# RWKV-6 state scan and gated FFN on one core: a new instruction order, with new bank, mask and transfer tables

## The chip, the cores and the metric

The kernel runs on one core of a Trainium2 chip. The metric is the time of the program on the device in microseconds; lower is better. Engines: PE is TensorE (matmuls; PEld is its weight load), DVE is VectorE, ACT is ScalarE, POOL is GpSimd, SP is SyncE, which here only issues transfers. POOL issues transfers too.

## The reference

The first half is a linear attention with a state of 48 x 48 per head, 4 batches, 8 heads, 768 steps; the second half a gated FFN without activation on 3072 rows.

```python
for t in range(S):
    cur = einsum('bhd,bhe->bhde', u[None] * kt, vt)
    y[:, :, t] = einsum('bhd,bhde->bhe', rt, state + cur)
    state = wt[:, :, :, None] * state + einsum('bhd,bhe->bhde', kt, vt)
# x: y as (3072, 384)
a = x @ w1          # 384 x 1024
b = x @ w2          # 384 x 1024
out = (a * b @ w3) @ w_out      # 1024 x 1024, 1024 x 384
```

## The kernel before

Time is cut into 6 chunks of 128 steps. A unit `t` is one chunk of one or two batches; there are 13: units 0 and 1 are chunk 0 of one batch each, unit 2 is chunk 0 of the other two batches, and units 3 to 12 are chunks 1 to 5 in pairs of batches. The steps of a unit, by the names of the order:

- `win`, `kin`, `rin`, `vin` load the rows of w, k, r and v. The transfers issued by POOL turn float32 into bfloat16 on the way (those of w do not). Unit 0 comes by SP into float32 tiles and is converted on chip (`kc`, `rc`, `vc`).
- `ln` and `cs` make the logarithm of w and its running sum over the chunk (a matmul with a triangle), `ne` and `e` the exponentials of it, `KRk` and `KRr` the scaled k and r. They are turned by 128 x 128 transposes on PE with an eviction (`trk` and `trke`, `trr` and `trre`) or by transposing transfers on SP (`dtk`, `dtr`). In the units of `RAW` (0, 1, 2, 3, 6) r is turned first (`trw`) and scaled by `KRw`, with factors made by `csT` and `et`.
- `m_t_b` multiplies turned k and r into a 128 x 128 score per head; the strict triangle is cut out by DVE from PSUM (`msk`), or, for the pairs in `POOL_MASK`, ACT copies (`mcp`) and POOL or DVE masks in SBUF (`maff`).
- The diagonal term is apart: `rk`, `ruk`, `dg` (sum over a head), `dv`. `ys` (state part) and `yi` (score part) sum into PSUM; `yb` adds `dv` and writes the rows of y. In the units of `Y_PE` a matmul `yd` adds `dv` and `ybc` copies.
- The rows are turned into `xT` by PE (`yt`, eviction `xT`) or, in `DMA_Y`, by two transposing transfers (`dty`).
- The state: `kv` is k times v, `T` adds the old state, `S` scales it by `pc`, `Sb` writes a bfloat16 copy. In `KV_WIDE` the product is made for pairs of heads, half as many matmuls, and `T` (or `S` in chunk 0) reads it in two halves of 64 partitions.

The FFN of a unit has four groups `g` (two for units 0 and 1): `a_t_g` and `b_t_g` are the matmuls with w1 and w2 (six of 256 columns), `asb` copies a to SBUF on ACT, `abT` multiplies by b from PSUM on DVE. Then `o_t_b` multiplies by w34 = w3 x w_out, `osb` evicts and `st` stores. w34 is made once on chip: `wt` turns w3, `w3Te` evicts, `wm` multiplies by w_out, `w34e` evicts. `warm` are matmuls on zeros. The rows of units 8 to 11 are loaded into the space of w3 and w_out once these are used up.

There is no scheduler: the text `ORDER` lists every step with its engine, `BANKS` gives each step its PSUM bank or its buffer, and the instructions of an engine stand in that order. Each engine works its own list in order and waits where an input or a buffer is not ready, and so do the queues: POOL's list has its transfers and its products, SP's list all stores and transposing transfers. Where a step of the order is a transfer, what stands behind it on that engine is issued later.

```python
ORDER = """
table@ACT zeros@DVE padlw@DVE win_0@POOL ones@DVE LT@POOL ln_0@ACT warm0@17 cs_0@PE ne_0@ACT win_1@POOL win_2@POOL
"""
```

Of the kernel before, what the change touches and what calls it, by code (L numbers as in the profile page):

```python
# [41 lines left out]
tk1=3 m1_0=0,1 M1_0=3 y1=0,1 yt1=2 kv1=3 a1_0=0 b1_0=6 sa1_0=0 a1_1=3 b1_1=2 sa1_1=1 o1_0=7 so1_0=2 cs2=0,1 ct2=3,4
tr2=5 tk2=6 m2_0=0,1 M2_0=1 m2_1=0,1 M2_1=2 y2=6,7 yt2=2 kv2=3 a2_0=5 b2_0=6 sa2_0=0 a2_1=7 b2_1=1 sa2_1=0 a2_2=5
b2_2=0 sa2_2=1 a2_3=7 b2_3=1 sa2_3=2 o2_0=5 so2_0=3 o2_1=6 so2_1=1 cs3=4,5 ct3=4,5 tr3=5 tk3=4 m3_0=2,3 M3_0=0
m3_1=4,5 M3_1=1 y3=0,1 yt3=0 kv3=2 a3_0=5 b3_0=6 sa3_0=2 a3_1=6 b3_1=7 sa3_1=2 a3_2=6 b3_2=4 sa3_2=1 a3_3=3 b3_3=2
sa3_3=0 o3_0=7 so3_0=2 o3_1=4 so3_1=0 cs4=4,5 tr4=4 tk4=5 m4_0=2,3 M4_0=2 m4_1=0,1 M4_1=3 y4=4,5 kv4=0,1 a4_0=4 b4_0=6
sa4_0=0 a4_1=2 b4_1=5 sa4_1=0 a4_2=7 b4_2=4 sa4_2=2 a4_3=0 b4_3=7 sa4_3=1 o4_0=5 so4_0=2 o4_1=4 so4_1=2 cs5=2,3 tr5=7
tk5=3 m5_0=2,3 M5_0=1 m5_1=6,7 M5_1=0 y5=0,1 yt5=6 kv5=6 a5_0=6 b5_0=7 sa5_0=0 a5_1=6 b5_1=2 sa5_1=0 a5_2=4 b5_2=1
sa5_2=2 a5_3=0 b5_3=2 sa5_3=1 o5_0=2 so5_0=3 o5_1=0 so5_1=0 cs6=0,1 ct6=0,1 tr6=0 tk6=1 m6_0=2,3 M6_0=3 m6_1=0,1
M6_1=2 y6=3,4 yt6=3 kv6=5 a6_0=5 b6_0=3 sa6_0=2 a6_1=3 b6_1=5 sa6_1=2 a6_2=4 b6_2=3 sa6_2=0 a6_3=0 b6_3=4 sa6_3=0  # L50
o6_0=0 so6_0=0 o6_1=3 so6_1=1 cs7=2,3 tk7=1 m7_0=2,3 M7_0=1 m7_1=6,7 M7_1=0 y7=0,1 yt7=1 kv7=5 a7_0=1 b7_0=5 sa7_0=2
# [12 lines left out]
kin_2@POOL padkr@DVE csT_0@PE rin_0@SP padr@DVE I128@POOL rin_2@POOL rin_1@POOL rc_0@ACT trw_0@PE et_0@ACT kin_0@SP  # L64
kc_0@DVE KRk_0@DVE ln_1@ACT mask1@DVE warm7@2 csT_1@PE pc_0@ACT rk_0@DVE cs_1@PE ne_1@ACT padet@DVE KRw_0@DVE ln_2@ACT
pc_1@ACT trk_0@PE trke_0@DVE kin_1@POOL warm7@2 m_0_0@PE u@SP csT_2@PE cs_2@PE w3_0@POOL vin_0@SP vc_0@DVE kv_0@PE
mcp_0_0@ACT ne_2@ACT uc@DVE ruk_0@DVE dg_0@DVE S_0@DVE rk_2@DVE mask@POOL vin_2@POOL w2_0@POOL KRk_2@DVE trw_2@PE
et_2@ACT dv_0@DVE KRw_2@DVE trk_2@PE trke_2@ACT KRk_1@DVE warm7@5 m_2_0@PE maff_0_0@DVE yi_0_0@PE yd_0@PE ruk_2@DVE
wt_0_0@PE wt_0_1@PE dg_2@DVE et_1@ACT wt_1_0@PE pc_2@ACT mcp_2_0@ACT maff_2_0@DVE trk_1@PE trke_1@DVE w1_1@POOL
vin_1@POOL m_2_1@PE trw_1@PE w2_1@POOL w1_0@POOL kv_2@PE wt_1_1@PE w3Te_0@ACT ybc_0@ACT w3Te_1@ACT win_3@POOL yt_0@PE  # L70
msk_2_1@DVE yi_2_0@PE yi_2_1@PE dv_2@POOL yd_2@PE ybc_2@ACT KRw_1@DVE m_1_0@PE xT_0@DVE rk_1@DVE wo@POOL ruk_1@POOL
b_0_0@PE yt_2@PE warm5@2 a_0_1@PE asb_0_1@ACT msk_1_0@DVE xT_2@DVE b_2_0@PE S_2@DVE yi_1_0@PE a_2_2@PE dg_1@DVE
w3_1@POOL dv_1@DVE a_2_3@PE yb_1@DVE yt_1@PE kv_1@PE xT_1@DVE b_2_2@PE asb_2_2@ACT abT_2_2@DVE b_2_1@PE b_1_1@PE
asb_2_3@ACT ln_3@ACT b_0_1@PE abT_0_1@DVE S_1@DVE a_1_0@PE a_0_0@PE asb_0_0@ACT abT_0_0@DVE a_2_0@PE asb_2_0@ACT
abT_2_0@DVE a_1_1@PE a_2_1@PE asb_1_1@ACT asb_2_1@ACT kin_3@POOL cs_3@PE abT_2_1@DVE ne_3@ACT b_1_0@PE wm_1@PE
asb_1_0@ACT b_2_3@PE abT_2_3@DVE Sb_0@DVE rin_3@POOL csT_3@PE et_3@ACT wt_2_0@PE wt_2_1@PE wt_3_0@PE pc_3@ACT
abT_1_0@DVE wm_0@PE wt_3_1@PE KRk_3@DVE trk_3@PE w3Te_2@DVE abT_1_1@DVE trw_3@PE KRw_3@DVE wm_2@PE w3_2@POOL Sb_1@DVE
w34e_1@ACT rk_3@DVE trke_3@ACT ruk_3@DVE m_3_0@PE msk_3_0@DVE m_3_1@PE w3Te_3@ACT wm_3@PE w34e_3@ACT vin_3@POOL
w34e_0@DVE wt_5_0@PE wt_4_0@PE wt_4_1@PE wt_5_1@PE ys_3@PE w3Te_5@ACT kv_3@PE yi_3_0@PE w34e_2@DVE w3Te_4@DVE wm_4@PE
w34e_4@ACT msk_3_1@DVE yi_3_1@PE dg_3@DVE dv_3@DVE yb_3@DVE wm_5@PE win_4@POOL ln_4@ACT w3_3@POOL wt_6_0@PE iw_4@ACT  # L80
Sb_2@ACT w34e_5@ACT wt_6_1@PE w3Te_6@DVE wt_7_0@PE wt_7_1@PE cs_4@PE e_4@ACT yt_3@PE w3Te_7@DVE xT_3@DVE T_3@DVE
wm_6@PE ne_4@ACT win_5@POOL kin_4@POOL S_3@DVE wm_7@PE ln_5@ACT cs_5@PE w34e_6@DVE a_3_1@PE pc_4@ACT iw_5@ACT
w34e_7@ACT KRk_4@DVE trk_4@PE e_5@ACT ne_5@ACT rin_4@POOL rw_4@DVE KRr_4@DVE trr_4@PE vin_4@POOL kv_4@PE rk_4@DVE
ruk_4@DVE asb_3_1@ACT dg_4@DVE o_0_0@PE o_2_1@PE T_4@DVE pc_5@ACT rin_5@POOL S_4@DVE kin_5@POOL trke_4@ACT trre_4@ACT
m_4_1@PE osb_0_0@ACT st_0_0@SP m_4_0@PE msk_4_0@DVE msk_4_1@DVE ys_4@PE win_6@POOL ln_6@ACT kin_6@POOL rin_6@POOL
vin_5@POOL KRk_5@DVE rk_5@DVE rw_5@DVE osb_2_1@ACT o_1_0@PE osb_1_0@ACT b_3_3@PE win_8@POOL vin_6@POOL dv_4@POOL
KRr_5@DVE yi_4_0@PE a_3_3@PE asb_3_3@ACT win_7@POOL win_9@POOL st_1_0@SP cs_6@PE ne_6@ACT Sb_3@ACT a_3_2@PE yi_4_1@PE
asb_3_2@ACT yb_4@DVE dty_4_1@SP b_3_1@PE trk_5@PE KRk_6@DVE abT_3_1@DVE csT_6@PE et_6@ACT kin_7@POOL pc_6@ACT rk_6@DVE
rin_7@POOL abT_3_3@DVE b_3_0@PE trke_5@ACT b_3_2@PE a_3_0@PE asb_3_0@ACT abT_3_0@DVE ruk_6@POOL trr_5@PE trre_5@ACT
trw_6@PE trk_6@PE o_2_0@PE m_5_1@PE m_5_0@PE KRw_6@DVE trke_6@ACT m_6_1@PE abT_3_2@DVE o_3_1@PE ruk_5@POOL dg_5@DVE  # L90
osb_2_0@ACT msk_5_1@DVE kv_6@PE kv_5@PE mcp_5_0@ACT m_6_0@PE mcp_6_1@ACT maff_5_0@DVE kin_8@POOL rin_8@POOL
msk_6_0@DVE ys_5@PE ln_7@ACT iw_7@ACT maff_6_1@POOL T_5@DVE T_6@DVE ln_8@ACT osb_3_1@ACT dv_5@POOL vin_7@POOL
vin_8@POOL o_3_0@PE dg_6@DVE osb_3_0@ACT cs_7@PE e_7@ACT dty_4_0@SP b_4_0@PE yi_5_0@PE yi_5_1@PE yb_5@DVE ne_7@ACT
pc_7@ACT win_11@POOL KRk_7@DVE a_4_0@PE asb_4_0@ACT dv_6@DVE b_4_1@PE a_4_2@PE Sb_4@ACT asb_4_2@ACT abT_4_0@DVE
cs_8@PE a_4_1@PE pc_8@ACT ys_6@PE b_4_3@PE yi_6_0@PE yt_5@PE e_8@ACT rw_7@DVE S_5@DVE KRr_7@DVE dtr_7@SP S_6@DVE
ne_8@ACT xT_5@ACT KRk_8@POOL a_4_3@PE yi_6_1@PE asb_4_3@ACT rk_7@DVE trk_7@PE win_10@POOL a_5_0@PE yb_6@DVE a_5_3@PE
b_4_2@PE rin_9@POOL asb_4_1@ACT abT_4_1@DVE yt_6@PE kin_9@POOL abT_4_3@DVE iw_8@ACT st_3_0@SP asb_5_0@ACT a_5_1@PE
# [692 lines left out]
```

## Time and profile before

| what | value |
|---|---|
| median of 3 runs | 164.85 us (164.43 to 165.8) |
| the profiled execution's own time | 164.84 us |
| its span | 163.1 us |
| granted TensorE clock | 1.0 |
| PE, DVE, ACT, POOL busy | 154.6, 125.2, 100.5, 97.8 us |
| HBM read, written | 27.98 MB, 4.72 MB |

The profile is of one execution. A row of the timeline gives start, time, engine, line and operation; neighbours of one kind are merged (x and their count), and the bracket behind it is idle time of the engine ahead of it with what ended it. A row of the chain gives start, time and what ran or was waited for. A PE matmul's time holds its way through the array, so its rate is read from the starts of a run of matmuls. The rows of DMA issues end with the microseconds from issue to landing.

### The profile page before, as it was taken

The numbers are of one execution on the slowest core, as the hardware profiler recorded it, in microseconds if no ns is written. First come the engines' busy times: TensorE is split into PE (matmuls) and PEld (weight loads), VectorE is DVE, ScalarE is ACT, GpSimd is POOL, SyncE is SP. The second block draws the span as 40 slices with busy tenths as digits, with TensorE's granted clock in tenths as the row PEclk, the third lists the DMA queues.
The fourth block names the chain that finished last, engine by engine and source line by source line (L and its number), as shares of the span: only waits on it lengthen the run. The fifth ranks groups of instructions, "written<-read, shape, count | busy, mean of one in ns | idle before, by whom it ended". The sixth has DMA issues, their size and how long they took to land.

```text
span 163.1 us, 4587 instructions
## 1 busy us (share of the span) xinstructions
PE 154.6 (95%) x1922; PEld 117.4 (72%) x1922; DVE 125.2 (77%) x202; ACT 100.5 (62%) x166; POOL 97.8 (60%) x90
## 2 busy tenths in 40 slices
PE   6977999999999999999999999999999999999990
...
GB/s 119 216 154 184 195 193 244 207 171 212 238 153 174 164 216 244 124 113 83 148 225 99 175 188 147 169 171 144 186 162 158 158 170 95 87 55 45 55 147 96
DMA packets 98837, 25.63 MB, mean 157 GB/s; under 512 B 90880, under 2 KB 96640, under 8 KB 98816
## 3 DMA queue, kind: packets, MB, share of 16 engines
...
q8 instruction: 15, 0.25, 0.7%
...
HBM read 27.98 MB, written 4.72 MB: 200 GB/s over the span
## 4 chain that ended last, share of the span: by engine, by line
PE 65%; DVE 14%; DMA 13%; issue 3%; POOL 2%; ACT 1%; DVEq 0%; POOLq 0%; ACTq 0%
PE banks L714 25%; PE banks L730 16%; DMA wo_bf<-in_moe_w_out_dram 8%; PE banks L380 7%; DMA win<-in_w_dram 5%; PE banks L551 3%; DVE dv L539 3%; DVE yb L614 2%; PE banks L371 2%; PE banks L596 2%; DVE abT L724 2%; PE banks L424 2%; PE banks L512 2%; PE banks L667 2%; DVE Mbf L570 1%
## 5 line engine op out<-in xcount | busy, mean ns | idle before, releaser
L714 PE MATMUL banks<-xT,w_bf 128*128 128x256 bf16 (+1 forms) x624 | 69.2, 264 | 0.7 <-DVE yb L614 0.4
L714 PEld LDWEIGHTS <-w_bf 128*128 128x128 bf16 x624 | 55.3, 98 | 8.2 <-issue 1.0
L719 ACT COPY a_sb<-banks 128x512 f32<-128x512 f32 x48 | 27.9, 589 | 25.8 <-PE banks L714 19.0
L724 DVE TENSOR_TENSOR abT<-a_sb,banks 128x512 bf16<-128x512 f32 x48 | 31.6, 682 | 14.9 <-ACT a_sb L719 7.9
L730 PE MATMUL banks<-w,abT 128*128 128x384 bf16 x192 | 33.8, 326 | 0.0
L730 PEld LDWEIGHTS <-abT 128*128 128x128 bf16 x192 | 18.2, 98 | 10.9
L570 DVE TENSOR_TENSOR Mbf<-banks,mask 128x1024 bf16<-128x1024 f32 x15 | 18.1, 1220 | 2.1 <-PE banks L551 2.1
L335 POOL DMA_DIRECT2D win<-in_w_dram x13 | 14.8, 1143 | 5.3 <-ACT NEt L441 3.2
L735 ACT COPY osb<-banks 128x384 f32<-128x384 f32 x21 | 10.0, 482 | 12.8 <-PE banks L730 12.8
L408 ACT ACTIVATE lw<-win 128x768 bf16<-128x768 f32 (+1 forms) x13 | 10.4, 796 | 8.5 <-DMA win<-in_w_dram 8.5
L530 DVE TENSOR_REDUCE dg<-ruk 128x16 f32<-128x768 bf16 (+1 forms) x13 | 11.5, 886 | 0.8 <-POOL ruk L524 0.7
L565 POOL TENSOR_SCALAR_AFFINE_SELECT Mbf<-Mbf 128x1024 bf16<-128x1024 bf16 x5 | 5.5, 1090 | 11.0 <-ACT Mbf L557 11.0
L380 PE MATMUL banks<-wo_bf,w3T 128*128 128x384 bf16 x64 | 11.6, 326 | 0.1
L335 POOL DMA_DIRECT2D kin<-in_k_dram x8 | 9.1, 1133 | 4.1 <-DMA win<-in_w_dram 2.8
L614 DVE TENSOR_TENSOR yb<-banks,dv 128x768 bf16<-128x768 f32 (+1 forms) x11 | 10.1, 919 | 1.8 <-PE banks L596 1.3
L441 ACT ACTIVATE NEt<-banks 128x768 bf16<-128x768 f32 (+1 forms) x13 | 9.9, 764 | 1.5 <-PE banks L424 1.1
L308 PE MATMUL banks<-zeros 128*128 128x512 bf16 x28 | 9.4, 488 | 1.3 <-DVE zeros L249 1.3
L335 POOL DMA_DIRECT2D rin<-in_r_dram x8 | 9.0, 1124 | 2.1 <-DMA w_bf<-in_moe_w_dram 1.5
L557 ACT CAST Mbf<-banks 128x1024 bf16<-128x1024 f32 x9 | 9.0, 1011 | 0.6 <-PE banks L551 0.5
L335 POOL DMA_DIRECT2D vin<-in_v_dram x8 | 9.2, 1148 | 0.2
L524 POOL TENSOR_TENSOR ruk<-rk,u_bc 128x768 bf16<-128x768 bf16 (+1 forms) x4 | 5.8, 1450 | 5.7 <-DVE rk L520 5.7
L380 PEld LDWEIGHTS <-w3T 128*128 128x128 bf16 x64 | 5.8, 98 | 3.6 <-DMA wo_bf<-in_moe_w_out_dram 0.2
(100 smaller groups left out, 244.9 us busy)
## 6 DMA issues: line engine op xcount, KB each, us to landing
out_dram<-osb SPq DMA_DIRECT2D x24, 192.0 KB, 3.9
...
kin<-in_k_dram POOLq DMA_DIRECT2D x7, 192.0 KB, 11.3
rin<-in_r_dram POOLq DMA_DIRECT2D x7, 192.0 KB, 11.2
vin<-in_v_dram POOLq DMA_DIRECT2D x7, 192.0 KB, 10.1
...
```

The source lines that it names most:

```text
L335: QUEUE[eng].dma_start(dst, src)
L380: nc.tensor.matmul(one(f"wm{fi}")[:, :DM], lhsT=w3T[fi % 2][:, gi, :], rhs=wo_bf[:, gi, :], start=(gi == 0), stop=(gi == FI - 1))
L408: nc.scalar.activation(LW[:, :, :D], ww, Act.Ln)
L441: nc.scalar.activation(N_.rearrange("t (b h) d -> t b (h d)", b=nb), cs_view(), Act.Exp, scale=-1.0)
L530: nc.vector.reduce_sum(dgs, ruks, axis=AX.X)
L570: nc.vector.tensor_mul(Mbf[bank[f"M{t}_{b}"]], mview(), mask.rearrange("s (j q) t -> s j q t", j=2))
L614: nc.vector.tensor_add(ybs.rearrange("t b (q e d) -> t e (b q) d", e=2, d=D), yview().rearrange("t e (x d) -> t e x d", d=D), dvs.rearrang ...
L714: nc.tensor.matmul(o[:, f, :], lhsT=wt[:, di, fi * P:(fi + 1) * P], rhs=x[:, di, :T], start=(di == 0), stop=(di == DI - 1))
L719: copier(eng)(a_sb[bank[f"sa{t}_{g}"]], one(f"a{t}_{g}"))
L724: nc.vector.tensor_mul(ab[:, g * per:(g + 1) * per, :T], sa.rearrange("p (f t) -> p f t", t=T), one(f"b{t}_{g}").rearrange("p (f t) -> p f ...
L730: nc.tensor.matmul(one(f"o{t}_{b}")[:, :DM], lhsT=ab[:, fi, b * C:(b + 1) * C], rhs=w34[:, fi, :], start=(fi == 0), stop=(fi == FI - 1))
L735: copier(eng)(osb[bank[f"so{t}_{b}"]], one(f"o{t}_{b}")[:, :DM])
```

## The change

Only the tables at the head of the kernel change; no step computes anything else.

```diff
-DMA_Y = {4, 9, 10, 11, 12}
+DMA_Y = {6, 8, 9, 10, 11, 12}
-POOL_MASK = {(0, 0), (2, 0), (5, 0), (6, 1), (7, 1), (9, 0), (10, 0), (11, 1), (12, 1)}
-Y_PE = {0, 2}
-KV_WIDE = {4}
+POOL_MASK = {(2, 1), (5, 1), (7, 0), (8, 1), (11, 1), (12, 0)}
+Y_PE = set()
+KV_WIDE = {1, 4, 10}
-wt0=5 wm0=1 wt1=2 wm1=3 wt2=7 wm2=6 wt3=0 wm3=0 wt4=3 wm4=3 wt5=7 wm5=7 wt6=6 wm6=1 wt7=3 wm7=7 cs0=0 ct0=0 tr0=1
+wt0=0 wm0=3 wt1=2 wm1=1 wt2=0 wm2=7 wt3=6 wm3=2 wt4=4 wm4=4 wt5=3 wm5=7 wt6=2 wm6=2 wt7=3 wm7=2 cs0=0 ct0=6 tr0=1
...
-table@ACT zeros@DVE padlw@DVE win_0@POOL ones@DVE LT@POOL ln_0@ACT warm0@17 cs_0@PE ne_0@ACT win_1@POOL win_2@POOL
+table@ACT zeros@DVE padlw@DVE padkr@DVE win_0@POOL ones@DVE ln_0@ACT LT@POOL win_2@POOL warm0@17 cs_0@PE rin_2@POOL
...
```

Steps that change their engine: from DVE to POOL `KRk_5`, `KRk_11`, `KRk_12`, `KRr_10`, `S_3`, `S_5`, `S_8`, `dv_6`, `dv_11`, `ruk_2`, `ruk_9`, `ruk_11`, `rk_11`, `rw_7`, `rw_9`, `rw_10`; from POOL to DVE `KRk_8`, `KRk_9`, `KRr_8`, `KRr_12`, `S_7`, `dv_2`, `dv_4`, `ruk_1`, `ruk_5`, `ruk_6`, `rk_12`, `rw_11`; from POOL to SP `win_9`, `win_10`, `win_11`; from ACT to POOL `rc_0`. Between ACT and DVE some evictions change sides: `osb` on DVE are 7 for 3, `w34e` 6 for 3, `Sb` 4 for 2, `xT` 2 for 6. DVE has 18 `msk` for 15 and 2 `maff` for 4.

POOL's list in the head (`kin_68` is `kin_1`, `w_bf` of 128x3x512 are the halves of w1 at L346 and of w2 at L350, `vin_73` is `vin_1`, `win_81` is `win_3`):

```order
+L335 DMA kin_68<-in_k_dram 128x8x48
+L346 DMA w_bf<-in_moe_w_dram 128x3x512 x2
 L350 DMA w_bf<-in_moe_w_dram 128x3x512
-L346 DMA w_bf<-in_moe_w_dram 128x3x512
+L524 TENSOR_TENSOR ruk_104<-rk_102,u_bc 128x768
+L565 AFFINE_SELECT Mbf_100<-Mbf_100 128x1024
 L335 DMA vin_73<-in_v_dram 128x8x48
 L350 DMA w_bf<-in_moe_w_dram 128x3x512
-L346 DMA w_bf<-in_moe_w_dram 128x3x512
 L335 DMA win_81<-in_w_dram 128x16x48
-L539 TENSOR_TENSOR dv_108<-vin_74,dg_106 128x768
 L354 DMA wo_bf<-in_moe_w_out_dram 128x8x384
```

Both halves of w1 now stand ahead of both of w2, and ahead of `vin_1`, the second transfer of w2, `win_3` and `wo` POOL has `ruk_2` and `maff_2_1`, where it had `dv_2` ahead of `wo` alone.

POOL's list where units 7 and 8 begin, before (`KR_94` are `KRk_8` and `KRr_8`, `ruk_104` is `ruk_8`; `w_bf` and `wo_bf` as targets are rows of later units):

```order
L335 DMA wo_bf<-in_v_dram 128x16x48
L335 DMA win_81<-in_w_dram 128x16x48
L445 TENSOR_TENSOR KR_94<-w_bf,NEt_90 128x16x48
L335 DMA win_80<-in_w_dram 128x16x48
L335 DMA w_bf<-in_r_dram 128x16x48
L335 DMA w_bf<-in_k_dram 128x16x48
L486 TENSOR_TENSOR KR_94<-rw_86,Et_88 128x16x48
L524 TENSOR_TENSOR ruk_104<-rk_102,u_bc 128x768
```

And of the change (`dv_108` is `dv_6`, `rw_87` is `rw_7`, `ruk_104` is `ruk_8`, `Sst_118` is `S_5`):

```order
L335 DMA win_78<-in_w_dram 128x16x48
L335 DMA wo_bf<-in_v_dram 128x16x48
L539 TENSOR_TENSOR dv_108<-vin_72,dg_106 128x768
L478 TENSOR_TENSOR rw_87<-rin_64,iw_85 128x768
L524 TENSOR_TENSOR ruk_104<-rk_102,u_bc 128x768
L689 TENSOR_TENSOR Sst_118<-Tst_116,pc_113 128x384
```

`KRk_8` and `KRr_8` are gone from POOL, and four products of units 5 to 8 stand there without a transfer between them.

DVE's list ahead of unit 6's scores, before (`abT_132` are unit 3's groups, `KRT_96` is `KRw_6`, `dg_107` is `dg_5`, `Mbf_98` is `msk_5_1`, `Mbf_99` `maff_5_0`, `Mbf_101` `msk_6_0`):

```order
L724 TENSOR_TENSOR abT_132<-a_sb_126,banks 128x512
L724 TENSOR_TENSOR abT_132<-a_sb_128,banks 128x512
L470 TENSOR_TENSOR KRT_96<-banks,ETt_92 128x1024
L724 TENSOR_TENSOR abT_132<-a_sb_127,banks 128x512
L530 TENSOR_REDUCE dg_107<-ruk_105 128x16
L570 TENSOR_TENSOR Mbf_98<-banks,mask 128x1024
L563 TENSOR_TENSOR Mbf_99<-Mbf_99,mask 128x1024
L570 TENSOR_TENSOR Mbf_101<-banks,mask 128x1024
```

And of the change (`yb_110` is `yb_4`, `Mbf_98` `msk_5_0`, `KRT_96` at L516 `trke_6` and at L470 `KRw_6`, `Mbf_100` and `Mbf_101` `msk_6_1` and `msk_6_0`):

```order
L614 TENSOR_TENSOR yb_110<-banks,dv_108 128x2x8x48
L724 TENSOR_TENSOR abT_132<-a_sb_127,banks 128x512
L570 TENSOR_TENSOR Mbf_98<-banks,mask 128x1024
L724 TENSOR_TENSOR abT_132<-a_sb_126,banks 128x512
L516 COPY KRT_96<-banks 128x1024
L470 TENSOR_TENSOR KRT_96<-banks,ETt_92 128x1024
L530 TENSOR_REDUCE dg_107<-ruk_105 128x16
L570 TENSOR_TENSOR Mbf_100<-banks,mask 128x1024
L570 TENSOR_TENSOR Mbf_101<-banks,mask 128x1024
```

`trke_6` and a third mask stand in this piece where ACT and a mask in SBUF had been, and `KRw_6` has more ahead of it.

More of the change, by code (lines that the diff above doesn't have):

```diff
@@ L42 @@
[L42 to L51, printed above, removed]
@@ L61 @@
 """
 ORDER = """
-table@ACT zeros@DVE padlw@DVE win_0@POOL ones@DVE LT@POOL ln_0@ACT warm0@17 cs_0@PE ne_0@ACT win_1@POOL win_2@POOL
[L64 to L97, printed above, removed]
@@ new lines @@
+padet@DVE KRw_0@DVE trke_0@ACT warm7@2 m_0_0@PE ln_2@ACT cs_2@PE ne_2@ACT csT_2@PE pc_2@ACT ruk_0@DVE dg_0@DVE
+vin_0@SP vc_0@DVE kv_0@PE msk_0_0@DVE KRk_2@DVE w1_1@POOL et_2@ACT ln_1@ACT trw_2@PE KRw_2@DVE warm4@2 trk_2@PE
+rk_2@DVE cs_1@PE yi_0_0@PE dv_0@DVE trke_2@ACT warm4@3 m_2_0@PE yb_0@DVE S_0@DVE m_2_1@PE w1_0@POOL wt_0_0@PE
+msk_2_0@DVE w2_1@POOL trw_1@PE ruk_2@POOL dg_2@DVE ne_1@ACT mcp_2_1@ACT csT_1@PE et_1@ACT Sb_0@ACT maff_2_1@POOL
+yt_0@PE xT_0@ACT yi_2_0@PE kv_2@PE KRk_1@DVE trk_1@PE trke_1@ACT wt_1_0@PE wt_1_1@PE w3Te_1@ACT yi_2_1@PE KRw_1@DVE
```

123 lines of the change are left out of this document (81 added, 42 removed).

## The prediction

> **What bounds the kernel now.** First the page's shares and its slices of TensorE (PE):
>
> ```profile
> PE 154.6 (95%) x1922; PEld 117.4 (72%) x1922; DVE 125.2 (77%) x202; ACT 100.5 (62%) x166; POOL 97.8 (60%) x90
> PE   6977999999999999999999999999999999999990
> ```
>
> PE is busy from slice 5 to the end. Then the table by stage (columns: the stretch, its length, busy time of PE, PEld, DVE, ACT and POOL, the granted clock, DMA share, GB/s):
>
> ```profile
> 33.40:53.82 20.42, 20.42 (x263) 15.20 (x264) 17.76 (x30) 13.83 (x23) 12.94 (x12) 1.00 1.99 190
> 53.82:74.00 20.18, 20.18 (x299) 15.45 (x297) 17.77 (x25) 17.12 (x28) 16.24 (x14) 1.00 1.83 167
> 74.00:84.30 10.30, 9.82 (x155) 8.28 (x153) 10.26 (x15) 8.23 (x16) 7.74 (x7) 1.00 1.38 161
> ```
>
> The clock is full, so no clock term is needed. From 33.40 on PE first idles in 74 to 84.3, where VectorE (DVE) is busy 10.26 of 10.30 us. The chain that ended last, a few pieces of it:
>
> ```profile
> 20.23 13.12 DMA wo_bf<-in_moe_w_out_dram
> ...
> 62.98 1.97 PE banks L714 x18
> ...
> 70.72 0.20 PE banks L586 x16
> ...
> 97.22 0.33 PE banks L633 x6
> ...
> 130.78 3.06 DVE dv L539
> ...
> 140.25 7.37 PE banks L714 x66
> 147.62 1.30 PE banks L730 x8
> ```
>
> It runs through the landing of `wo` at 33.35, then PE, then DVE up to 140 and PE to the end. But a piece of the chain is no loss: PE had other work beside that 3.06 of DVE. What PE lost is read from its starts. One L714 matmul takes 1.97/18 = 0.109 us, so a group of six 0.66; a `yt` takes 0.33, a `ys` 0.20, an `o` 1.30.
>
> ```profile
> 79.80 1.47 PE L714 MATMUL banks<-xT,w_bf 128*128 128x256 bf16 x12
> 81.64 0.81 PE L714 MATMUL banks<-xT,w_bf 128*128 128x256 bf16 x6 [0.37 <-DVE yb L614]
> 82.29 0.50 PE L633 MATMUL banks<-I,yb 128*128 128x128 bf16 x6
> 82.91 0.81 PE L714 MATMUL banks<-xT,w_bf 128*128 128x256 bf16 x6
> ...
> 134.51 0.37 PE L586 MATMUL banks<-Sbf,KRT 64*128 64x48 bf16 x16
> 135.03 2.78 PE L714 MATMUL banks<-xT,w_bf 128*128 128x256 bf16 x24
> ...
> 138.05 3.13 PE L714 MATMUL banks<-xT,w_bf 128*128 128x256 bf16 x25
> ```
>
> 79.80 + 12 x 0.109 = 81.11, but the next starts at 81.64: 0.53 lost. 82.29 + 0.33 against 82.91: 0.29. 134.51 + 0.20 against 135.03: 0.32. 138.05 + 1.97 for three groups against 140.25, where the chain goes on: 0.23. Together **1.37 us**, nearly all that waits cost behind 40 us. Ahead of them stand two stretched DVE instructions:
>
> ```profile
> L689 DVE TENSOR_TENSOR Sst<-Tst,pc x5: 552/557/1997, 50.2 to 87.1; 128x384 f32<-128x384 f32 x5
> 78.08 1.76 POOL L445 TENSOR_TENSOR KR<-w_bf,NEt 128x768 bf16<-128x768 bf16 x1 [1.91 <-ACT NEt L441]
> 131.37 1.63 POOL L520 TENSOR_TENSOR rk<-rin,kin 128x768 bf16<-128x768 bf16 x1
> 138.19 0.96 DVE L539 TENSOR_TENSOR dv<-vin,dg 128x768 bf16<-128x768 bf16 x1
> ```
>
> `S_6` (L689, at 78.3) needs 0.55 us and took 2.00 while GpSimd (POOL) ran `KRk_8`; `dv_11` took 3.06 while POOL ran `rk_12`, where another `dv` takes 0.96. I call this a port wait: 1.45 and 2.1 us of DVE.
>
> **Part 1: the head, to 39.1 us: 0.** Unit 2's rows go ahead of unit 1's and `w1` ahead of `w2`, but the set of transfers ahead of `wo` on POOL's queue is the same, and the three behind it (`w3_1`, `kin_3`, `rin_3`) are the same too. `wo` needed 13.12 us from issue to landing; its own 1024 x 384 values of two bytes are 4.1 us at the stage's 190 GB/s. The rest is backlog, so its landing follows the sum of bytes, not the order. Behind it:
>
> ```profile
> 24.08 1.16 POOL L335 DMA_DIRECT2D rin<-in_r_dram  x1
> rin<-in_r_dram POOLq DMA_DIRECT2D x1, 192.0 KB, 14.5
> 38.66 0.62 PE L465 MATMUL banks<-I,rin 128*128 128x128 bf16 x8
> 39.11 1.46 PE L380 MATMUL banks<-wo_bf,w3T 128*128 128x384 bf16 x8
> ```
>
> `rin_3` lands at 24.08 + 14.5 = 38.6; `trw_3` starts at 38.66, and `wm_2` behind it at 39.11. Both orders have the same PE work ahead of `wm_2`, but for `yd_0`, `yd_2`, one warm-up matmul and half of `kv_1`'s matmuls, under 1 us, which the changed kernel saves. As `trw_3` starts with the landing, that saving is swallowed. Nothing can be gained here unless bytes move faster; what can be lost is rival D. `rc_0` on POOL stands in no row: it costs between nothing, under the backlog, and about one POOL product (1.6); I take nothing, as 5 us and more of backlog stand behind it. `S_1` in two halves costs DVE at most one more `S` (0.55), and as the head ends with a landing this is nothing.
>
> **Part 2: PE's own work behind 39.1: -0.3.** `yt_6` and `yt_8` go, since these units' rows now come by transfers, and `yt_4` returns: one `yt` less, 0.33. `kv_10` in 8 wide matmuls for 16 narrow ones is about even.
>
> **Part 3: the waits named above: -1.4.** `KRk_8` leaves POOL and `dv_11` leaves DVE, so neither pair can meet again. The gain is less only if other pairs take their place (rival C).
>
> **Part 4: DVE from 53 to 71 us: +1.0.** DVE gets three masks more (two `maff` fewer), four `osb` more, three `w34e` more and a second half of `T_10`, against four `xT` and several products fewer: by row durations some 3.5 us more behind the first `wm`. Spread over 120 us this is nothing, but it is not spread. Rows for the sum:
>
> ```profile
> L570 DVE TENSOR_TENSOR Mbf<-banks,mask 128x1024 bf16<-128x1024 f32 x15 | 18.1, 1220 | 2.1 <-PE banks L551 2.1
> 62.44 0.55 DVE L445 TENSOR_TENSOR KR<-kin,NEt 128x768 bf16<-128x768 bf16 x1
> 62.91 0.68 DVE L724 TENSOR_TENSOR abT<-a_sb,banks 128x512 bf16<-128x512 f32 x1
> 63.50 0.55 DVE L520 TENSOR_TENSOR rk<-rin,kin 128x768 bf16<-128x768 bf16 x1
> ```
>
> Back to back, the next starts 0.08 before the end (62.44 to 62.91, 62.91 to 63.50): 0.47 for a product, 0.60 for an `abT`, and so 1.14 for a mask and 0.88 for a `dv`, as which I count `dg` and `yb` too. From `T_3` to `KRw_6` the changed order has 3 masks, 4 `abT`, `dg_4`, `dv_4`, `yb_4`, `trke_6` and `KRw_6` (taken as `abT`) and 13 of the size of a product: 3.4 + 2.4 + 2.6 + 1.2 + 6.1 = 15.7 us. PE from `m_4_0` to `m_6_1`, which waits for `KRw_6`, has four `o` (5.2), eight groups (5.3), five transposes (0.45 each, 38.66 to 39.11; 2.3) and small pieces of `cs`, `m`, `ys`, `yi` and `yt` (about 2.2): 15.0. DVE starts level, as it has just made `KRr_4` for `trr_4`, and so comes 0.7 late. Behind it stands a wait for POOL: `rw_7`, a product of about 1.65, ahead of `KRr_7`. I take 1.0 for both. Below: 0, if `T_3` and `rk_4` run earlier, as their inputs allow. Above: 2.5, with one port wait of 1.45 besides.
>
> `win_4` now goes ahead of `w3_2`: twice `rin`'s 192 KB, 2.0 us at 190 GB/s, on a landing that PE has so far met with a little to spare. 0 to 0.6; I leave it inside the 1.0.
>
> **What is hidden.** ScalarE loses three `mcp`, `rc_0` and evictions and was 62% busy: nothing. `win_9` to `win_11` go to SP's queue, behind stores and `dtr_7`; these rows are needed over 10 us later, and if SP held them up by that much, `cs_9` would pay the excess. `dty_6` stands behind `dtr_7` and `st_3_0`; `a_6_0` comes a dozen PE steps later. The end (last `o`, `osb`, store) has the same form.
>
> **Sum.** The profiled execution took 164.84 us (163.1 of span) beside a median of 164.85, so no correction. 164.84 + 0 - 0.3 - 1.4 + 1.0 = **164.1**, 0.4% less. About 1% is what a measurement of this kernel can tell from no change.
>
> **Rivals.**
> A. No new wait: 164.84 - 1.7 = 163.1, or 162.8 if the head gains a little. For it: PE lost nothing from 33.40 to 74 with DVE already at 17.77 of 20.18. Against it: 15.7 us of DVE for 15.0 of PE.
> B. The change does not do what it says: waits of the old size come back at other places. 164.84 - 0.3, with a little either way 164.3 to 165.3. For it: the same engines stay as full.
> C. Slower: POOL has 28 tensor instructions reading SBUF behind the first `w1`, where it had 25, and from 53 to 82 us DVE has nothing to spare, so a port wait there goes to PE in full. Two of the size seen cost 1.45 + 2.1 = 3.5: 164.1 + 3.5 = 167.6. It decides from 2.4 us of such waits. Against it: the order places `KRk_5`, `maff_5_1`, `S_3` and `dv_5` beside masks, `T` and `abT`, which read a PSUM bank, and no such row is stretched now.
> D. POOL is late with `wo`: `ruk_2` and `maff_2_1` now stand ahead of `vin_1`, `w2_0`, `win_3` and `wo`. If `m_2_1` keeps its time, `wo` is issued 1 to 2 us later than now; about half of its backlog of 9 us can be lost before a landing moves, and from there each microsecond is paid in full. 3 us give 167.
>
> By the Trainium skill, "SBUF — State Buffer", section "Who interferes with whom", a VectorE instruction with two SBUF inputs contends with a GpSimd instruction that reads SBUF, and the later one fully blocks. By that rule alone three more such readers speak against this change, and for C's time; the two stretched rows agree with it.
>
> **Chances.** The forecast 0.40, A 0.23, B 0.20, C 0.11, D 0.06. Faster by over 1% (under 163.2): A and a little of the forecast, 0.25. Slower by over 1% (over 166.5): C and D, 0.17. The rest, 0.58. The range goes from 162.7 to 166.8: A's lower end, and on the other side C and D left out for the most part.
>
> **What would show it.** Part 1: `wm_2` starts at 39.1, within 0.4. Part 2: seven `yt`. Part 3: no `S` and no `dv` on DVE over 1 us. Part 4: `m_6_1` behind a gap of about 1 us near 69. I am wrong if PE waits elsewhere by more than 1 us in all, or if `wo` lands behind 34.

## The result and the profile after

The changed kernel takes **170.97 us** (median of 4 runs, 168.94 to 171.75) where the kernel before takes 164.64 beside it: 1.0334 times as long, 95% interval 1.0276 to 1.0391. The prediction was 164.1, with a range from 162.7 to 166.8. The kernel is **slower by 3.3%**, and the time lies outside the range. (Medians are over all runs of a kernel; a ratio leaves disturbed runs out, and none is given where too few are left.)

The profiled run took 168.94 us, the shortest of the four, with a span of 167.1. Its shares, PE's slices and the granted clock:

```profile
PE 154.4 (92%) x1898; PEld 117.4 (70%) x1899; DVE 134.3 (80%) x207; ACT 94.2 (56%) x155; POOL 100.0 (60%) x91
PE   7979699999999999999999949996799999999991
PEclk9999999999999999999999999999689999999999
```

In the kernel before PE was full from slice 5 to the end. Now slices 24 and 28 to 29 are not, and behind the second hole the clock is below full. By stages, first the three that the prediction showed, then the two holes and the stretch behind the second:

```profile
33.40:53.82 20.42, 20.42 (x270) 14.74 (x270) 17.52 (x29) 13.87 (x21) 10.29 (x9) 1.00 1.95 187
53.82:74.00 20.18, 20.18 (x319) 15.89 (x314) 19.69 (x29) 14.76 (x24) 18.57 (x16) 1.00 2.72 160
74.00:84.30 10.30, 10.30 (x112) 8.96 (x111) 9.61 (x17) 8.77 (x15) 7.54 (x7) 1.00 1.58 177
90.00:100.00 10.00, 7.81 (x96) 5.63 (x93) 9.86 (x13) 4.79 (x10) 8.22 (x7) 1.00 1.42 191
110.00:118.00 8.00, 5.44 (x50) 4.11 (x49) 8.00 (x8) 4.31 (x8) 6.31 (x5) 1.00 1.34 117
118.00:122.00 4.00, 3.76 (x15) 2.10 (x15) 2.10 (x4) 1.99 (x3) 2.41 (x2) 0.58 0.36 95
```

Up to 90 us PE is as full as before or fuller (10.30 for 9.82 in the third row), though DVE is at 19.69 of 20.18 from 53 to 74. From 90 to 100 and from 110 to 118 PE loses 2.2 and 2.6 us, with DVE busy 9.86 of 10 and 8.00 of 8; then the clock is at 0.58 for 4 us. The kernel before has PE busy for the whole of both stretches, and DVE less:

```profile
90.00:100.00 10.00, 10.00 (x133) 8.37 (x133) 8.25 (x13) 7.46 (x15) 9.99 (x9) 1.00 1.59 167
110.00:118.00 8.00, 8.00 (x130) 5.97 (x127) 7.44 (x13) 5.89 (x11) 6.57 (x6) 1.00 1.72 165
```

PE's rows at the holes (the bracket is idle time ahead, and what ended it), `yt_7`, then `cs_12` and `o_7_0` with `b_8_1`'s first matmuls:

```profile
98.92 0.51 PE L633 MATMUL banks<-I,yb 128*128 128x128 bf16 x6 [2.19 <-DVE yb L614]
118.24 0.49 PE L424 MATMUL banks<-lw,LT 128*128 128x384 bf16 x2 [2.56 <-DVE yb L614]
118.56 2.65 PE L730 MATMUL banks<-w,abT 128*128 128x384 bf16 x8
```

Both times PE waits for a `yb` on DVE: `yt_7` needs its rows, and `cs_12` the bank that `yb_9` still reads. What stands ahead of the two `yb` on DVE, and what POOL runs beside it:

```profile
93.62 1.99 DVE L524 TENSOR_TENSOR ruk<-rk,u_bc 128x768 bf16<-128x768 bf16 x1
95.54 2.23 DVE L539 TENSOR_TENSOR dv<-vin,dg 128x768 bf16<-128x768 bf16 x1
97.91 0.96 DVE L614 TENSOR_TENSOR yb<-banks,dv 128x768 bf16<-128x768 f32 x1
...
114.02 3.30 DVE L478 TENSOR_TENSOR rw<-rin,iw 128x768 bf16<-128x768 bf16 x1
117.24 0.94 DVE L614 TENSOR_TENSOR yb<-banks,dv 128x768 bf16<-128x768 f32 x1
```

```profile
93.51 1.69 POOL L524 TENSOR_TENSOR ruk<-rk,u_bc 128x768 bf16<-128x768 bf16 x1 [1.70 <-DVE rk L520]
95.17 1.79 POOL L539 TENSOR_TENSOR dv<-wo_bf,dg 128x768 bf16<-128x768 bf16 x1
...
113.66 1.64 POOL L520 TENSOR_TENSOR rk<-w_bf 128x768 bf16<-128x768 bf16 x1
115.26 1.63 POOL L445 TENSOR_TENSOR KR<-w_bf,NEt 128x768 bf16<-128x768 bf16 x1
```

`ruk_10` and `rw_12` are products of 0.55 us, `dv_7` of 0.95. They took 1.99, 3.30 and 2.23: each started 0.1 to 0.4 us behind the start of a POOL product. `ruk_10` ended 0.4 behind the end of `ruk_9`, when `dv_8` had already begun; `rw_12`, which started beside `rk_11`, ended only behind `KRk_11` too. That is 1.44 + 2.75 + 1.28 = 5.5 us of DVE, right ahead of the two steps that PE waits for. It is rival C's mechanism, some 40 us later than where the prediction put it.

### The profile page after: what moved, and what is told of

Same layout as the page of the kernel before. It is cut to its first block, busy times and chain, and to the rows that moved or that the text cites. A ratio compares the mean times of both kernels' runs of the same rounds, so it can differ in the third digit from the quotient of the medians.

```text
span 167.1 us, 4566 instructions
## 1 busy us (share of the span) xinstructions
PE 154.4 (92%) x1898; PEld 117.4 (70%) x1899; DVE 134.3 (80%) x207; ACT 94.2 (56%) x155; POOL 100.0 (60%) x91
## 4 chain that ended last, share of the span: by engine, by line
PE 73%; DVE 9%; POOL 7%; DMA 5%; issue 3%; ACT 0%; DVEq 0%; POOLq 0%
PE banks L714 34%; PE banks L730 17%; PE banks L380 6%; DMA w_bf<-in_moe_w_dram 5%; PE banks L551 3%; PE banks L596 2%; PE banks L424 2%; PE banks L371 2%; PE banks L512 1%; POOL win L335 1%; DVE abT L724 1%; DVE dv L539 1%; POOL rin L335 1%; POOL kin L335 1%; PE banks L586 1%
## 5 line engine op out<-in xcount | busy, mean ns | idle before, releaser
L719 ACT COPY a_sb<-banks 128x512 f32<-128x512 f32 x48 | 26.9, 593 | 23.1 <-PE banks L714 21.4
L730 PE MATMUL banks<-w,abT 128*128 128x384 bf16 x192 | 35.7, 334 | 0.0
L570 DVE TENSOR_TENSOR Mbf<-banks,mask 128x1024 bf16<-128x1024 f32 x18 | 21.6, 1218 | 1.5 <-ACT lw L408 0.8
L735 ACT COPY osb<-banks 128x384 f32<-128x384 f32 x17 | 8.1, 481 | 17.5 <-PE banks L730 17.5
L614 DVE TENSOR_TENSOR yb<-banks,dv 128x768 bf16<-128x768 f32 (+1 forms) x13 | 11.6, 894 | 2.5 <-issue 1.5
L335 POOL DMA_DIRECT2D win<-in_w_dram x10 | 11.4, 1139 | 3.5 <-DMA wo_bf<-in_moe_w_out_dram 2.2
L524 POOL TENSOR_TENSOR ruk<-rk,u_bc 128x768 bf16<-128x768 bf16 x4 | 6.8, 1706 | 4.5 <-DVE rk L520 4.5
L539 POOL TENSOR_TENSOR dv<-wo_bf,dg 128x768 bf16<-128x768 bf16 x4 | 6.3, 1566 | 5.2 <-DVE dg L530 5.2
L424 PE MATMUL banks<-lw,LT 128*128 128x384 bf16 x24 | 6.0, 326 | 3.1 <-DVE yb L614 2.6
L565 POOL TENSOR_SCALAR_AFFINE_SELECT Mbf<-Mbf 128x1024 bf16<-128x1024 bf16 x4 | 4.4, 1110 | 7.4 <-ACT Mbf L557 7.4
```

What stands on the lines that cost most here:

```text
L335: QUEUE[eng].dma_start(dst, src)
L424: nc.tensor.matmul(o[:, b, :], lhsT=LT, rhs=LW[:, b * H:(b + 1) * H, :D], start=True, stop=True)
L570: nc.vector.tensor_mul(Mbf[bank[f"M{t}_{b}"]], mview(), mask.rearrange("s (j q) t -> s j q t", j=2))
L614: nc.vector.tensor_add(ybs.rearrange("t b (q e d) -> t e (b q) d", e=2, d=D), yview().rearrange("t e (x d) -> t e x d", d=D), dvs.rearrang ...
L719: copier(eng)(a_sb[bank[f"sa{t}_{g}"]], one(f"a{t}_{g}"))
L730: nc.tensor.matmul(one(f"o{t}_{b}")[:, :DM], lhsT=ab[:, fi, b * C:(b + 1) * C], rhs=w34[:, fi, :], start=(fi == 0), stop=(fi == FI - 1))
```

## The experiments

Four theories went into them. **P** (T1 in the first texts): products of DVE that wait for products of POOL ahead of a step that PE waits for. **Q**: transfers that land late on the queues. **T3**: the clock alone. **T2**: the order as a whole is longer, and what is won is lost again. Times are medians in us; the kernel before ran beside each at 164.9 to 165.1.

| kernel | median (runs) | ratio to before, 95% interval |
|---|---|---|
| changed | 170.97 (4) | 1.0334 (1.0276 to 1.0391) |
| e1, `rk_11`, `KRk_11` to DVE | 169.91 (4) | 1.0297 (1.0234 to 1.0361) |
| e2, `ruk_9`, `dv_8` to DVE | 176.35 (4) | 1.0668 (1.0610 to 1.0726) |
| e3, e1, e2 and `dv_9` to DVE | 174.28 (4) | 1.0542 (1.0475 to 1.0609) |
| e4, matmuls on zeros in the wait | 169.28 (4) | 1.0243 (1.0188 to 1.0298) |
| e6, `win_9` to `win_11` on POOL | 171.14 (4) | 1.0356 (1.0282 to 1.0430) |
| e7, y of 6 and 8 by PE | 171.95 (4) | 1.0398 (1.0318 to 1.0478) |
| e9, `rw_12` late | 169.86 (4) | - |
| e10, `dv_7` early | 171.81 (4) | 1.0383 (1.0302 to 1.0465) |
| e11, e9 and e10 | 167.72 (4) | 1.0145 (1.0080 to 1.0209) |
| e17, `win_11` behind `dtk_9` | 170.85 (6) | 1.0303 (1.0249 to 1.0356) |
| e15, e11 and e17 | 164.73 (10) | 0.9981 (0.9951 to 1.0011) |
| e12, e11 and `vin_12` early | 167.79 (4) | - |
| e13, e12 and e17 | 164.66 (12) | 0.9967 (0.9940 to 0.9993) |
| e14, e13 and `kin_9` first | 165.42 (12) | 1.0005 (0.9973 to 1.0037) |
| e16, e17 and `vin_12` early | 168.10 (4) | 1.0168 (1.0110 to 1.0227) |
| e5, new head, old rest | 166.46 (10) | 1.0088 (1.0051 to 1.0125) |
| e8, before with two products to DVE | 164.10 (10) | 0.9950 (0.9908 to 0.9992) |

### Products off POOL: e1, e2, e3

```diff
 e1: -rk_11@POOL +rk_11@DVE  -KRk_11@POOL +KRk_11@DVE
 e2: -ruk_9@POOL +ruk_9@DVE  -dv_8@POOL +dv_8@DVE
 e3: e1, e2 and -dv_9@POOL +dv_9@DVE
```

> The changed kernel with rk_11 and KRk_11 on VectorE instead of GpSimd. Theory T1 (two pairs of waits between VectorE products and GpSimd products, at 93 to 97 and 111 to 117 us, with the fall of the granted clock behind the second, are what the change lost): rw_12 takes 0.55 instead of 3.30 us, cs_12 follows a_8_0 within 0.5 us instead of 2.77, the clock stays full and o_7_0 takes 1.3 instead of 2.45; 3.5 to 4.5 us less than the changed kernel's 170.97, so 166.5 to 167.5. Rival T2 (the new order as a whole is longer, and the wait only shows where): cs_12 comes earlier, but later waits take up the gain; less than 1 us, 170 or more. Rival T3 (only the clock costs): as T1 here.

> The changed kernel with ruk_9 and dv_8 on VectorE instead of GpSimd. T1: ruk_10 takes 0.55 instead of 1.99 and dv_7 0.95 instead of 2.23, yt_7 follows b_6_2 within 1 us instead of 2.31 plus; VectorE has 1.35 us of work more itself. 1.0 to 2.0 us less than 170.97, so 169.0 to 170.0, if the later wait at 116 stays. T2: nothing, 170.5 to 171.5, as slack ahead of the wait at 116 swallows it. T3 (only the clock costs): nothing either.

> The changed kernel with rk_11, KRk_11, ruk_9, dv_8 and dv_9 on VectorE instead of GpSimd. T1: no VectorE product over 1.3 us between 90 and 118 us, PE without a wait over 0.6 there; VectorE has 2.4 us of work more and is the next bound. 163.5 to 166.5: at the kernel before (164.6) or a little on either side. T2: 169 or more.

In e1 the wait at `cs_12` and the fall of the clock behind it went, as P says, but only 1.1 us came of it. The wait at `yt_7` stays (2.13 us), and now the clock falls behind that one, to 0.50 from 102 to 104; and PE waits elsewhere, here at `m_12_1`:

```profile
138.82 0.40 PE L551 MATMUL banks<-KRT 64*128 64x128 bf16 x8 [1.61 <-DMA KRT<-KR]
```

`m_12_1` starts at 138.82, in the changed kernel at 138.87. The gain lies within the two intervals. e2 and e3 came out over 6 and 7 us longer than P had them, and e2 longer than any theory. The wait at `yt_7` is shorter (1.4 us in e2), but a far longer one comes (PE, e2, `m_9_0`):

```profile
111.90 1.04 PE L551 MATMUL banks<-KRT 64*128 64x128 bf16 x16 [4.93 <-DMA KRT<-KR]
```

Without its two products POOL issues `rin_11`, `rin_12` and `kin_11` at 93.3 to 96.8 instead of 96.9 to 100.4. They lie beside `dtr_8`, `dtr_9`, `win_11` and `dtk_9` on SP's queue, and `dtk_9` lands at 111.85 instead of 104.87. So moving a product to another engine also moved the transfers behind it, and these experiments do not test P by itself; the next ones leave the engines alone. They brought Q.

### The clock: e4

```diff
 asb_8_0@ACT st_5_0@SP
-cs_12@PE
+warm4@12 cs_12@PE
```

> The changed kernel with 12 matmuls on zeros (0.215 us each, 2.6 us in all, into the bank of o_7_0) on TensorE between a_8_0 and cs_12, where it otherwise idles 2.77 us. They leave the wait itself as it is, and only keep TensorE busy. T1: the granted clock stays full from 116 to 124, o_7_0 takes 1.3 and b_8_1 0.66; 1.5 us less than 170.97, so 169.0 to 170.0, and the rest of the loss stays. T3 (only the clock costs): 166 or less. T2: nothing, 170.5 or more.

The wait stays and is filled (PE, e4: the zeros, `cs_12`, `o_7_0`):

```profile
120.47 2.54 PE L308 MATMUL banks<-zeros 128*128 128x512 bf16 x11
122.98 0.48 PE L424 MATMUL banks<-lw,LT 128*128 128x384 bf16 x2
123.30 1.46 PE L730 MATMUL banks<-w,abT 128*128 128x384 bf16 x8
```

`o_7_0` shows 1.46 instead of 2.65, and from the start of `cs_12` to that of `kv_10` PE takes 2.27 us (122.98 to 125.25) instead of 3.95 (118.24 to 122.19): 1.7 less. The median falls by 1.7 too, though the two intervals still touch. So the fall of the clock behind a wait is a cost of its own of about that size. T3, that it is all of the loss, is out: beside it PE idles 2.19 + 2.56 us in the changed kernel's profile.

### Two parts undone: e6 and e7

```diff
 e6: -win_9@SP +win_9@POOL  -win_10@SP +win_10@POOL  -win_11@SP +win_11@POOL
 e7: -DMA_Y = {6, 8, 9, 10, 11, 12}  +DMA_Y = {9, 10, 11, 12}
     -dty_6_1@SP dty_6_0@SP +yt_6@PE xT_6@ACT   -dty_8_1@SP dty_8_0@SP +yt_8@PE xT_8@ACT
```

> The changed kernel with win_9, win_10 and win_11 on GpSimd's queue, at the same places of the list, instead of SP's. Theory Q (on SP's queue these rows stand between the transposes dtr_9 and dtk_9 and hold them, and with them SP's list, up; part of the loss): dtk_9 takes under 6 us from issue to landing instead of 8.3, 1 to 2 us less than 170.97, so 169 to 170. Rival T1 (only waits between VectorE and GpSimd products count): as GpSimd issues three transfers of 1.2 us more, its products come later and meet others; 170 to 172.

> The changed kernel with y of units 6 and 8 turned on TensorE again (yt_6 and yt_8, 0.33 us each, and an eviction by ScalarE), as in the kernel before, instead of by four transposing transfers. Theory Q: SP has four transposes fewer, 5.3 us of its issue time; transposes behind them land earlier, and the gain is at least the 0.7 us that TensorE pays: 169.5 to 171. Rival T1: 171.3 to 172, the price of TensorE alone.

Neither gains. In e6 PE waits 1.2 us at `yt_7`, but 1.6 more at `ys_7` and 2.6 at `cs_12`. e7 is 1 us longer, about TensorE's price, but inside the two intervals; in it `asb_4_0` evicts `yt_6`'s bank in place of `a_4_0`'s, with the same amount of work. Undone alone, neither the rows on SP nor the y by transfers brings the loss back.

### Order alone: e9, e10, e11

These keep every engine and every transfer, and only let `yb_9` and `yb_7` pass the products that nobody waits for yet.

```diff
 e9:  -abT_7_2@DVE rw_12@DVE          +abT_7_2@DVE
      -abT_8_0@DVE dtr_10@SP          +abT_8_0@DVE rw_12@DVE dtr_10@SP
 e10: -abT_5_1@DVE o_5_0@PE           +abT_5_1@DVE dv_7@DVE o_5_0@PE
      -yi_7_1@PE Sb_6@DVE osb_4_1@ACT ruk_10@DVE dv_7@DVE a_6_2@PE
      +yi_7_1@PE osb_4_1@ACT a_6_2@PE
      -yb_7@DVE yt_7@PE abT_6_0@DVE   +yb_7@DVE yt_7@PE abT_6_0@DVE Sb_6@DVE ruk_10@DVE
 e11: both
```

> The changed kernel with one step moved on VectorE: rw_12, which nobody needs before 127 us, behind abT_8_0 instead of ahead of yb_9. No step changes its engine, and GpSimd's and SP's lists stay. Theory P (what costs is a product that waits for GpSimd's products in front of a step that TensorE waits for): yb_9 starts by 114.7 instead of 117.2, cs_12 follows a_8_0 within 0.6 us, the clock stays full there, kv_10 starts 3 us earlier or more; 1 to 3 us less than 170.97, so 168 to 170, since m_12 may come to wait for its transposes as in the run with rk_11 and KRk_11 on VectorE. Rival (that wait is set by the transposes or transfers, not by the product): cs_12 waits as before, 171.

> The changed kernel with three steps moved on VectorE: dv_7 ahead, behind abT_5_1, and Sb_6 and ruk_10 behind yb_7 and abT_6_0, so that no product stands between GpSimd's ruk_9 and dv_8 and yb_7. Theory P: yt_7 follows b_6_2 within 0.6 us instead of 2.31, and no fall of the clock behind it; 1.5 to 3 us less than 170.97, so 168 to 169.5, with the wait at cs_12 as it was. Rival (VectorE as a whole is late there: 9.86 us busy of 10 from 90 to 100): the wait moves to the next step, 170.5 to 171.5.

> Both: rw_12 behind abT_8_0, and dv_7 ahead, Sb_6 and ruk_10 behind yb_7. Theory P: both waits and both falls of the clock go, 4 to 6 us in all of the profiled run's loss; 165 to 167.5. It stays above the kernel before if m_12 waits for transposes that stand beside the transfer of unit 12's rows. Rival: 169 or more.

e10 gains nothing: 0.8 us more, inside the two intervals. e9's runs lie too far apart to tell, one at 166.64 and three from 169.64 to 170.19. In each the named wait goes (nothing over 0.3 us at `cs_12` in e9, nor at `yt_7` in e10), while the other stays: 4.1 us at `yt_7` in e9, 2.6 at `cs_12` in e10. And in e10 a wait that the changed kernel does not have comes in place of the one at `yt_7`, at `m_9_0`:

```profile
107.50 0.62 PE L551 MATMUL banks<-KRT 64*128 64x128 bf16 x16 [2.46 <-DMA KRT<-KR]
```

Both together give 167.72, **3.2 us less**, half of the loss. Both waits that P names are gone, but the one at `m_9_0` is there in e11 too (PE; then SP's list, then the stretch behind):

```profile
106.99 0.62 PE L551 MATMUL banks<-KRT 64*128 64x128 bf16 x16 [2.22 <-DMA KRT<-KR]
```

```profile
96.45 0.53 SPq L335 DMA_DIRECT2D win<-in_w_dram  x1
97.07 3.64 SPq L506 DMA_TRANSPOSE KRT<-KR  x1
```

```profile
108.00:110.00 2.00, 2.00 (x7) 0.88 (x6) 0.66 (x1) 1.53 (x2) 1.88 (x2) 0.50 1.58 223
```

Here `m_9_0` waits 2.2 us for `dtk_9`. That transpose stands behind `win_11` (384 KB, landed at 102.2), takes 3.64 us to issue and lands at 106.95; behind the wait the clock is at 0.50.

### The queue: e12, e13, e14

```diff
 e12: e11 and -osb_9_1@ACT vin_12@POOL +osb_9_1@ACT   -kin_12@POOL +kin_12@POOL vin_12@POOL
 e13: e12 and -dtr_9@SP win_11@SP dtk_9@SP +dtr_9@SP dtk_9@SP win_11@SP
 e14: e13 with kin_9 ahead of kin_10 on POOL; on DVE KRk_9 first, rk_10 behind yb_7 and abT_6_0
```

> As the run with both moves, and vin_12 behind kin_12 on GpSimd's queue (about 114 us) instead of behind S_9 and dv_11 (about 133), so that its transfer does not lie beside dtr_12's. Theory Q for the end (a row transfer of GpSimd's queue beside a transpose delays it by 3 us and more): m_12_1 follows o_9_1 without a wait; 0.5 to 2 us less than the run with both moves alone, 164 to 166. Rival (the transposes at 113 to 119, dtr_10 and dtk_10, are held up by it instead): no gain or a loss.

> As the run with both moves and vin_12 early, and on SP's queue win_11 (384 KB, landing 5 to 10 us after issue) behind dtk_9 instead of ahead of it. Theory Q (what is left of the loss, and of the spread between runs, are landings: dtk_9 comes behind win_11, and m_9 waits 2.3 to 5 us for it in the runs in which the transfers lie badly, with a fall of the clock behind it): dtk_9 lands before 103 in every profile, m_9_0 without a wait; median 163 to 165, and no runs above 167. Rival (the spread has another cause): median 166 to 168 as without it, single runs from 163.5 to 169.

> As the run before it, and kin_9 ahead of kin_10 on GpSimd's queue, KRk_9 and rk_9 ahead of rk_10 on VectorE, so that KRk_9 doesn't wait for kin_9's landing (1.1 to 1.8 us of VectorE in the runs in which ruk_9 and rw_12 were moved). Theory Q: yb_7 and yt_7 come without a wait also where transfers lie badly; median 162.8 to 164.5, below both kernels. Rival (rk_10 and what hangs on it comes too late, or landings at other places set the time): 165 or more.

e12 gave 167.79, but its 4 runs lie from 163.62 to 169.01 and tell nothing of `vin_12`; its shortest run, the one profiled, had no wait at `m_9_0`. e13 gave 164.66, with one of 12 runs above 165.3 (167.14, where none was expected above 167). e14 gave 165.42, not better: `kin_9`'s late landing holds `KRk_9` up by over 1 us in e15 as well, which is level with e13 (DVE, e15):

```profile
94.80 0.56 DVE L445 TENSOR_TENSOR KR<-w_bf,NEt 128x768 bf16<-128x768 bf16 x1 [1.28 <-DMA w_bf<-in_k_dram]
```

### How it divides: e15, e16, e17

```diff
 e15: e11 and -dtr_9@SP win_11@SP dtk_9@SP +dtr_9@SP dtk_9@SP win_11@SP
 e16: the changed kernel with this swap and e12's move of vin_12
 e17: the changed kernel with this swap alone
```

> The changed kernel with the moves on VectorE (rw_12, dv_7, Sb_6, ruk_10) and win_11 behind dtk_9, but vin_12 at its old place behind S_9 and dv_11. If vin_12's place counts (its transfer beside dtr_12's, as in the run with rk_11 and KRk_11 on VectorE): m_12_1 waits 1 to 2.6 us behind o_9_1, 165.5 to 167. If not, as the run with vin_12 early: 164.2 to 165.2.

> The changed kernel with the two moves on the queues alone (win_11 behind dtk_9, vin_12 behind kin_12), and VectorE's list as it is. If the waits between products and the late landings are two losses that add: the waits at yt_7 (2.3) and cs_12 (2.8) and a fall of the clock (1.1 to 1.5 each) stay, 4 to 6 us above the kernel before, 168.5 to 170.5. If the landings alone made the loss, 165 to 166.

> The changed kernel with one swap on SP's queue and nothing else: win_11 behind dtk_9 instead of ahead of it. Behind the moves on VectorE this swap brought 3.0 us (167.7 to 164.7). If it is a loss of its own: 167.5 to 169. If it counts only once TensorE no longer waits for yt_7 (in the profile of the changed kernel dtk_9 lands at 104.87, just ahead of m_9_0 at 105.22): 170 to 171.5, the changed kernel's time.

e15 equals e13, so `vin_12`'s place does not count. From e11 to e15 one swap of two neighbours on SP's list brings **3.0 us**. SP's rows and `m_9_0` in e15, beside those of e11:

```profile
96.94 1.89 SPq L506 DMA_TRANSPOSE KRT<-KR  x1
98.92 0.53 SPq L335 DMA_DIRECT2D win<-in_w_dram  x1
```

```profile
105.06 0.62 PE L551 MATMUL banks<-KRT 64*128 64x128 bf16 x16
```

`dtk_9`, issued at the same time, lands at 101.78 instead of 106.95, and `m_9_0` waits for nothing. The clock is full again, and PE nearly so; the two slices below 9 hold waits of 0.92 and 0.58 us (page of e15):

```profile
PE   6978699999999999999999798999999999999991
PEclk9999999999999999999999999999999999999999
```

The same swap alone (e17) gains nothing: as long as PE is held up at `yt_7`, `dtk_9` is in time (in the changed kernel it lands at 104.87, and `m_9_0` starts at 105.21). e16 came to 168.10, by another way than expected: the issue of `vin_12` (1.15 us) stands ahead of `rk_11` on POOL, so `rk_11` starts at 117.82, and `rw_12` passes before it (DVE, e16):

```profile
117.05 0.80 DVE L478 TENSOR_TENSOR rw<-rin,iw 128x768 bf16<-128x768 bf16 x1
```

Its wait at `cs_12` is gone and the one at `yt_7` stays (2.99 us), so e16 is one more removal of the second meeting, and no test of the queues.

Read together, the runs put the loss into two holes of about 3 us each. The one at `cs_12` has one cause, `rw_12` held up ahead of `yb_9`: without that e16 is 2.75 us below e17. The one behind `yb_7` has two, one behind the other: `ruk_10` and `dv_7` ahead of `yb_7`, and `dtk_9` behind `win_11`. e10 takes away only the first of these and e17 only the second, and neither gains; with both gone the gain is 3.0 (e11 to e15) to 3.4 us (e16 to e13).

### The prediction's own parts: e5 and e8

```diff
 e5: the changed kernel's order and banks up to wm_2, behind it the kernel before's
 e8: the kernel before with -KRk_8@POOL +KRk_8@DVE  -rk_12@POOL +rk_12@DVE
```

> One part alone: the changed kernel's steps up to wm_2 (38 us, with their banks, w1 ahead of w2, unit 2's rows ahead of unit 1's, no yd, wide kv_1), and behind wm_2 the order of the kernel before, word for word, with its queues and its banks. Theory H (the new head gains its 1.1 us and the new order behind it loses all): wm_2 starts at 38.0 us, no wait over 0.6 us behind it, 163.3 to 164.0 beside 164.9 for the kernel before. Rival (an early head is no gain, as DVE or the transfers of later rows set the pace behind it): 164.5 to 165.3.

> The kernel before with KRk_8 and rk_12 on VectorE instead of GpSimd, so that S_6 and dv_11 cannot meet them. The prediction's part 3 (these two meetings cost TensorE 1.37 us): S_6 takes 0.55 and dv_11 0.96 us, the four short waits behind them go, 163.4 to 164.1 beside 164.9. Rival (VectorE's two products more, 0.47 each, and the next late step take up the gain): 164.5 to 165.2.

e5 does not settle the head: at the seam PE waits 1.4 us ahead of `wm_4`, which neither whole kernel does (and `w34e_2` evicts a bank that `wt_5` has overwritten, the work being the same). e8 is 0.8 us shorter than the kernel before: that is what taking the two products away from POOL is worth, with DVE's two more products in it.

## Why the prediction was wrong, point by point

**Part 1 (the head, 0): right in size, not in its tolerance.** `wm_2` started at 37.82 in the changed kernel's profile, outside 39.1 +- 0.4. But the same head ran in 17 profiled kernels, with `wm_2` from 37.82 to 39.60, mean 38.6, against 39.11 and 38.91 in the two profiles with the old one: a gain of 0.4, and a spread of 1.8 between runs. `wo` landed at 31.7, and `rin_3`, whose landing the prediction made the end of the head, at 37.2; `trw_3` followed at 37.38.

**Part 2 (-0.3): right.** 36 transposes, that is 5 x 6 + 2 x 3, are seven `yt`:

```profile
L633 PE MATMUL banks<-I,yb 128*128 128x128 bf16 x36 | 3.2, 219 | 2.2 <-DVE yb L614 2.2
```

**Part 3 (-1.4): these two meetings went, the size is not confirmed.** `S_6` takes 0.55, `dv_11` is on POOL. e8 gains 0.8 where the part has 1.37. That is less than all of it: DVE has two products more there, and `dv_11` still takes 1.47 beside POOL's `S_10`, which ran from 130.57 beside the 3.06 in the kernel before as well and which the prediction did not see. The condition at the part's end, that no other pairs take their place, decided; its sign, no `dv` on DVE over 1 us, failed with `dv_7`'s 2.23.

**Part 4 (+1.0 at `m_6_1`): not there.** `m_6_1` follows `o_3_1` (67.33 + 1.30 = 68.63) at once:

```profile
68.73 0.62 PE L551 MATMUL banks<-KRT 64*128 64x128 bf16 x16
```

DVE was indeed full there, 19.69 of 20.18. But the estimate of 15.7 for 15.0 assumed that both start level. DVE began `T_3` at 51.58, 1.9 us ahead of unit 4's first scores on PE (53.47), and was done with `KRw_6` at 68.16, 0.5 ahead of `o_3_1`'s end. This is the case that the part itself gave for its lower bound of 0.

**The step that failed** is the weighing of rival C. Its mechanism came: DVE's stretched instructions ahead of `yb_7` and `yb_9` hold 5.5 us, beyond the 2.4 from which it decides. But the prediction looked for meetings only from 53 to 82 us, where DVE's share was highest, found masks, `T` and `abT` beside POOL's products, and gave C 0.11. `ruk_9` and `dv_8`, `rk_11` and `KRk_11`, two POOL products back to back each time, stand 40 us later; three of these four (all but `dv_8`) the change itself moved from DVE to POOL, as its own list of engine changes said. The Trainium skill, "SBUF — State Buffer", section "Who interferes with whom", which the prediction cited, agrees: each of the three DVE products started later than the POOL product that it met, and outlasted it.

**Two terms were put at nothing.** First, "what is hidden" asked when `win_9` to `win_11` are needed, not what stands behind them on SP's list: `dtk_9` behind `win_11` costs 3.0 us once the other waits are gone (e11 to e15). Second, "no clock term is needed" holds only while PE does not wait: e4 puts the fall behind one wait at about 1.7.

**The sum.** From the changed kernel to e11 3.25 us go, from e11 to e15 2.99, and e15's 164.73 is level with the kernel before. So the loss is these faults, and without them the change is about even. That e15 also lies near the forecast of 164.1 is partly luck. With the sizes that the runs showed for the parts (0.4 from the head, 0.3, 0.8, nothing lost at `m_6_1`) the sum is 164.84 - 1.5 = 163.3, 1.4 below e15. Two waits of 0.92 and 0.58 us are left in e15's profile; whether they are that difference was not tested. e13, 0.3% under the kernel before (interval 0.1 to 0.6%), and e8, 0.5% (0.1 to 0.9%), are the shortest versions found.
